# Two layers of spectral filter and bilinear unit on one core: who makes the first sums, smaller last steps, and a new order

## The chip, the cores and the metric

The kernel runs on one core of one Trainium2 chip. The metric is the device time of one execution in microseconds; a comparison takes the median of several runs. Engines: TensorE (PE in the profile) multiplies, VectorE (DVE), ScalarE (ACT) and GpSimd (POOL) work on elements, and SyncE (SP) issues nearly all transfers. Each engine does its instructions strictly in the order of its own queue.

## The reference

x has 2048 rows and 512 columns in float32. Twice over, two blocks are added to it:

```python
def _A_ref(x, w_r, w_i):
    X = rfft2(x, axes=(-2, -1))
    return irfft2(X * (w_r + 1j * w_i), s=(S, D), axes=(-2, -1))

def _B_ref(x, w_gate, w_up, w_down):          # F = 1792
    h = einsum("bsd,df->bsf", x, w_gate) * einsum("bsd,df->bsf", x, w_up)
    return einsum("bsf,fd->bsd", h, w_down)

x = x + _A_ref(layernorm(x), w_r0, w_i0)
x = x + _B_ref(layernorm(x), w_gate, w_up, w_down)
x = x + _A_ref(layernorm(x), w_r0, w_i0)      # the same weights again
x = x + _B_ref(layernorm(x), w_gate, w_up, w_down)
```

Both layers use the same weights. The layer norm has no scale and no shift.

## The kernel before, in words

x stays in SBUF for the whole run, as xs: 128 partitions, 16 tiles t of 512 columns. A layer goes through four stages.

*Forward.* For each tile t, `stats` and `rstd` make the reciprocal deviation rs (VectorE's bn_stats, two small steps on ScalarE, two on VectorE for each tile). Tiles are normalized in groups: the list G0 (line 18) gives the groups of the first layer, g2_ (line 1100) those of the second half between the layers. `fwd_rest` scales the twiddle tw by rs on ScalarE, folds the tile's columns on GpSimd (fo; tiles 2, 5, 8, 11 and 14 of layer 0 skip this and are combined by VectorE afterwards), multiplies (tp, eight matmuls), and copies the result into E. Tile 15, the last, is copied in two pieces, so that the groups that come first (FAST, line 104) need not wait for the whole.

*Middle.* E is worked through in 16 groups g. `middles` makes for each group a sum and a difference fs of two halves of E over all 16 tiles: on VectorE for the groups in FAST, on GpSimd for the others. CUTS (line 105) divides the sums of groups 0 to 2 into an early part (tiles 0 to 11) and a late one (12 to 15), so that the early part can be made before the last tiles are there. TensorE turns fs into features dp, ScalarE copies them to zs, TensorE multiplies across (zp), VectorE, ScalarE and GpSimd apply the filter (wq, loaded in eight pieces; jz and qp are its intermediate products), TensorE goes back (vq), and ScalarE stores into E. Groups are taken in pairs, (0), (1, 2), (3, 4) up to (15); dp of a pair is one step of 32 matmuls in the queue. A product without use (wp, "idle") stands between the last tile and the first features.

*Inverse.* For each tile `inv` multiplies (yi), forms vs, multiplies by the inverse twiddle (yo), and VectorE adds the result to xs in three steps. Then come the statistics of the second layer norm; `build_x` turns the normalized tiles (tq) and writes the operands xA and xS of the unit.

*Bilinear unit.* The hidden width is worked through in 14 slices ft, for the first eight tiles (h0 = 0) and the last eight (h0 = 8). `unit` forms gate and up products in a scheme with seven products instead of eight (gx, gy, gw, gz, gv), in one go of 512 columns (half = None) or in two halves of 256; a product is six matmuls. `down` forms the down products of two slices at once with seven products (ex to ez), and adds to xs. Where that scheme does not pay (first half of layer 0, and slices 0 and 1 at the end of layer 1), three matmuls db make each tile's down product directly, and VectorE adds it to xs (lines 868 to 887). The list seq (line 1029) says in which order slices come; the second half of layer 0 ends with slices 1 and 0 in halves, that of layer 1 with slice 1 whole and slice 0 in halves. The last eight tiles are stored at the end (lines 1110 and 1111), one transfer of 256 KB each.

*Order.* The functions only register operations. `Plan.order` sorts all 4887 of them by one written list: ORDER holds the sequence (as packed differences of indices), PLACES the buffer slot of each tile as it first appears. An engine's queue is the part of the sequence that belongs to it. The numbers called due have no effect on it. All instructions pass one helper, so the profile gives line 303 for every one; tiles are told apart by their names.

Of the kernel before, what the change touches and what calls it, by code (L numbers as in the profile page):

```python
# [17 lines left out]
G0 = [(0,), (1,), (2,), (3,)] + [(t, t + 1) for t in range(4, 16, 2)]  # L18
# [10 lines left out]
def consts():  # L29
# [74 lines left out]
FAST = (0, 1)  # L104
CUTS = {g: ((0, 12), (12, 16)) for g in range(3)}
# [6 lines left out]
UFIRST = 5.0  # L112
UNITS = ((7.5, 17.4, 15.0), (7.2, 16.9, 16.9)), ((7.2, 16.9, 14.5), (7.2, 14.5, 14.5))
# [3 lines left out]
    'c-l=`2Y3}#)1GtgO%Dkz5a|*+ibyp<igZMpNReW}f_zf^M35>dRT2FJ73?4&iV#phP(Tncbiqc6h#(y)0YV5#_RRmz>?ZzCp1pVP*;A*y^UiFDqNzMZQ68V<+vq%(p|f0)u5m2g#C6UjIzus'  # L117
    '(NQVC8YG}W~<){RmV1t%QxUTaRu8i+%Xi30ajx)Iwe&6IuxX<Gl++V=6V)(p^)^aqJvYF%xEZPgW3dK=1Doy7&9y64{h+SNpLYV0kTg+XKEP7SOo(z?vEBLfnV;QH|G?&H0sVy_lH`81U)un'
    'j4f%zQHVbM$0Er}7w`C0s0hLL44uR#m5d{?FeTmy4E?7uWcqNOx`W%G3|jybkq4(94q5xc6Q>;BAlWByo3p$5fbrsI4KJ?qkT^t>G_T;lRNe-=m5LF~IcBw)~UKiAjx9h^*`VeNPt4JjvL#S'
    'pcot1P=@UaRZ1r{$bvpaZNG#&1h|&{lv^W%x4Hp}9N)t#9Mp=XfPQh*>@U6H<$zT%5vEGMV5{WMJqXT)*pGEHqr1e&Xgh+d8fa87{}lX%uVIJz04K`iM@W@Wj$@{3u<7WUg{e8o?9v{066dj'  # L120
    'yKXmoi7J_s)O&^lpgxsv3JA`rEOdfmSLbdS?>d$uBVHq!}xqc_feYu;-ipi9`0vAFTMqppaERK??HmM<J8yr63fXOQEQ$?rLf=U`5jn~fy52X<2P}41{PKV`@CQGGFK%f`jhWi+J}A(agz4D'
    '4O%mLdU=vUr`hN@hFyw956ABxcqdNN88*SZ3~lA<N3_;bJ2QHv@zeNx4A&(*Igjg3)w9ey*t`$_=!f6CSfu@jn`#DgY2F!X2DM#O30-y<s4477)?LHWcPIPfJE*R9K+gB5loHjxrLDBt$*EM'
    'Fc0&URXuE^t$$TAcpvQ(-dppZct6|;?cy@(5>a!3e_6>gozsli#u>OZA9jks$W1OXl<{%%z7^fc4m-?y{+F@Vf6P01#&1fjkN83{L5+4{upRn|nS=#{x;#CWgG@WN+#R$3u-#icPdEA4tRol'
    'b0|8(`nZFqK-k74CD@IC|i@8TSeRJ;8Ot9I4<bofO>d{>9|dvLBIMh~i~GHr`qL-{*8in%vnw@snN2e>~hH=R6pks5Lz^h;ph>a*w=iv(`RZkOua(~xxxP8QZR53$JpaasTm`UUORAfb)e=_'
    'fkgLay?;h*I>7`S9E(^d^slO+vHmYvwhY0~?N^dUP4B3-~#Vc$1^3xypV!r&CY97i$^l>=G{_=SEOnJD$3Di+CKpj`n8g`Jn4=U&Z}g9t$sd2jeY0kGtaNVQCaBYAW}F_Zw=AS@(O7*-<POU'
    'PAYh5LkRe-EoY`H#1F?H=$rFy<|3ErW$;JAE8;mYlmOgToi>&UrvXX1R2E+4{=?L&&B-?ubE}O<{~kxf#=^zd1$T0g7ya~3iJPp>zo^GzQ*@`be^_)Einb!xFSYWpfdET8)ME=8U9DDcfNP8'
    'ZHfCi-hVB00{{4h%Nj#9@a%j18bIH{J4^EgoU9V>(Q}2&89eDj!(AsU{$=40k?bhMtmt}_Z@Cy#jwK2;G@{3*l;igC8ux;Y0`kn|H*J;|hZSz4vKY77g{cMB+y_rLz><?Li82vs#8wWHc%D@'
    'mKIE;i+t8yMpXW$(Ol`Lc_4FRJ(NvFrr5R?Sxe8CdSNmshk{?6daaeaeJwzGsQj0w??}g<)NtuXVhgtTq8|M*y);8ivGTRj@iIwUbSvMW~yWgBsyQ&KNw2C|i=$b~UYFWOI%3lJ_=EigiUKF'
    'BJkd;{0F?gc^nu=AgaE;AgT(?mKRpHHOzo8gah2G(*-dfugdbmgTX-qP7k%DKVSUjRT;;QtG;k(Q{{tY{xV<x#o_{9_>5$`)!jMB_qG|N3==JL~A+{k`ry5YL>Qt**mt|Hnl@@e==hDMa9+('
    '%f&(u=OSS?At1JKQ{4jNgm#v?cH&f)=@P#ui1YMQAV2x0|Cl(TDJNLmlY|dKvl_ekS<ThlaY|rj<(mVfTzlQyg!JIoGR?0|U|GqffFTRb>hV9wJ(6<+iEJ*YOh9!w70u)s;nh)v%UWMGfG>W'  # L130
    'kjYp8tvAZ8g8#SjP_C(KZz&fa~Gn12vT3pi*(k3{3(6GO~GmMF-se_(1=AESYmDEDtD@9W^*eN-eQB@V7HL*K@$zk7yOmhPk9E_=F#X=99k#|>3?XFsHV#_VU4+;>m2>uR&&++(mbVn=s4ev'
    'c}iLf<Vth3@O{WD1>JRZC2bYT^9<c(7MoqJCADxrnM^Jl(f-zAQ<IvyosfJb+R9~JZEFJgU^Hyk!0z4v*43weJPg<|*&Plg7W{zrfx!GQWtdzJxm+U_m+Z<~+1)-cIzyRWg2v}#q3&)2OElc'
    'UIo>tyZjXCyv9}58RSvkD0vZ0nMo%9_39h}};FY!wRWf^F<D<PNY%TbZVE@M~So;+`>kqG{l@XV`;#T7DW^N5O5ebb6YZcCu=*|L*_HzT^e1!F}evUT}y{pm`{@qKYu2y1ho|j@zbG*B5UeP'
    'sQ;#|+S!h7wHUUB&ABUWPFCJwvicE9%*eDiKAn#=G$4sCS4#NJj$`KXRufHl5iVY1h85<wsF{TW^lD>$&+>t^o;(<<%qSbDw#u2zc#QKw_{IGc)?H;@zE+{ldl2wLDh50tM1ANkD-Q)9c+>t'
    '|o_`q)VN#}f&Tu<v@q?T10Edzr>!j+wSUFQ!6o%5>9RE>FTrdm!_@c;3iXM2xBC=7q9>AKk$Q4Bbt`ymzeF{0MJ@ZR<tTzK|{Gi<U5Kz|d2k;QYOI6Xc$THkBN_;Y;sX>+==hxOdT%fjlnr5'
    'WCbHZ}%W35A$-lEY-BaQC`HX`P|wL(Y<ZLi1)o(c7R%20lfQ9^}TUke|smq{t5K@6*F}7viKISj4W5MhJ~SL;`1SDhq-dNtsRDup&)*RsI4b+eFyEVM9dPM@5lGE-ty1|C$kU0{EJv-nB|SZ'
    'D!=i=xI9HniJUU}Jb&T_nGTr$jIH3ELmVvUW!My2#YW?7s-o~o*jh6Gq-)%%_~Ns)-F#iWI80@{9g(Z@fljdQ8t`|YhlTY!moM=5?DIzp%(;d8>9`-}8o(EiXkOEqKUDrB?4@eJbgMu{!a>9'
    'r?opk;WU^f=aIj{GCdnq9=TR$u68z&W9&6gL(e*^Oy<u@jfI~j!JW1_z^bD>5-yO&^_=SMiBI@bqAmI0ZsVe`aoOGo2j-(knz5+6l8aUM&%69#f752f&jv|Kig`fW$qx`>K{0i{$I{4Z{;PS'
    '^24-GJ-G9|e^<~uwUol3u1)G@$>1aREbTnwj@Y^FW=nEjyUexm1ZG1Gmt2Dz2feBmrVpgq23;cTBH;_c;`oP)DRA$x64UGa1%3j()-u0CO31{ZMUE7vqs5iN7HmsQ+vNN;JTChWTfbnyiX4?'
    '2tQP;kC}?uv;7*1f^2;cL$#?@OfPx{FGD5=^)eeM~pqM4Us;u#P3_8+shr($Kb`N#w^Kv8V)P9vM8G-$D-KXV6{{>)!)M*{I{kqklOw5T9`x4SlWp`|^L|<k&+Jz9-=v64Cs8*JwWe8jaDjI'  # L140
# [132 lines left out]
def kernel(ctx: ExitStack, tc: tile.TileContext, x, wf, wc, wb, dfwd, tf, ti, mid, out):  # L273
# [733 lines left out]
    for layer in range(2):  # L1007
        dcs["i"] = load_di()
        idle(IDLE[layer])
        for gs in TWOS:  # L1010
            middles(gs, E, dcs["f"], W, lambda g: t0 + BOFF + BSTEP * g, SWAPS[layer])
# [156 lines left out]
```

## Time and profile before

| | |
|---|---|
| median of 3 runs | 1037.28 us (1037.04 to 1037.31) |
| the profiled execution | 1037.49 us |
| its span in the profile | 1035.7 us |
| TensorE busy | 1020.6 us, 99% |
| VectorE, GpSimd, ScalarE busy | 793.7, 745.8, 419.7 us |
| granted clock of TensorE | 1.00 throughout |

The span goes from the first to the last instruction of the trace; the device time holds a little more on either side. TensorE is the engine that is nearly always busy, so idle time on the others counts only where TensorE waits for them. Matmul ends are modelled and overlap a little: the distance from start to start is the better price of one.

### The profile page before, as it was taken

How to read it: one execution, taken by the hardware profiler on the slowest of the kernel's cores; microseconds unless marked ns; L12 is line 12 of the kernel's file. 1: busy time of each engine (PE TensorE's matmuls, PEld its weight loads, DVE VectorE, ACT ScalarE, POOL GpSimd, SP SyncE). 2: the span in 40 equal slices, each digit the busy share in tenths (PEclk: the TensorE clock that was granted, in tenths of full speed). 3: DMA queues.
4: the chain of work that ended last, by engine and by line, in shares of the span. 5: the costliest groups of instructions: out<-in, count | busy, mean ns of one | idle time of the engine just before them, and what ended most of it. 6: DMA issues, size and time to landing. Idle time of an engine off the chain costs nothing.

```text
span 1035.7 us, 18681 instructions
## 1 busy us (share of the span) xinstructions
PE 1020.6 (99%) x6544; PEld 878.8 (85%) x6544; DVE 793.7 (77%) x1533; ACT 419.7 (41%) x989; POOL 745.8 (72%) x950
## 2 busy tenths in 40 slices
PE   8999999999999999999999999999999999999998
PEld 6777988888888888889987789888888888888897
DVE  7779777678866677778878796888887766677788
ACT  6679534434432422332376693222333421222231
POOL 6968999999997675655798466554779953456571
PEclk9999999999999999999999999999999999999999
DMA  9720677767785675455290005536796365565442
GB/s 346 304 80 19 225 241 237 251 186 254 221 272 185 211 253 188 152 203 206 87 386 10 9 5 207 202 123 220 217 255 198 103 205 191 204 244 204 153 142 82
DMA packets 129468, 193.65 MB, mean 187 GB/s; under 512 B 39264, under 2 KB 50784, under 8 KB 127328
## 3 DMA queue, kind: packets, MB, share of 16 engines
q1 hardware_dynamic: 129232, 192.21, 55.1%
q8 instruction: 52, 0.85, 0.3%
q14 instruction: 40, 0.33, 0.1%
q10 hardware_dynamic: 144, 0.26, 0.1%
HBM read 145.52 MB, written 46.92 MB: 186 GB/s over the span
## 4 chain that ended last, share of the span: by engine, by line
PE 93%; DVE 4%; DMA 1%; ACT 1%; issue 1%; POOL 1%; SPq 0%; DVEq 0%; ACTq 0%
PE gz L303 15%; PE gx L303 15%; PE db L303 8%; PE gw L303 7%; PE gy L303 7%; PE gv L303 7%; PE ex L303 5%; PE ez L303 5%; PE ew L303 3%; PE dp L303 3%; PE zp L303 3%; PE ev L303 3%; PE vq L303 3%; PE ey L303 3%; PE tp L303 3%; DVE xs L303 2%
## 5 line engine op out<-in xcount | busy, mean ns | idle before, releaser
L303 PE MATMUL gx<-xA,wt 128*128 128x512 f32 (+1 forms) x756 | 175.5, 368 | 0.0
L303 PEld LDWEIGHTS gx<-xA,wt 128*128 128x128 f32 x756 | 130.4, 189 | 21.3 <-ACT s L303 0.2
L303 POOL TENSOR_TENSOR sf<-q,sf 128x256 fp32r<-128x256 f32 x99 | 73.2, 744 | 84.4 <-ACT sf L303 79.9
L303 POOL TENSOR_TENSOR sf<-cc,sf 128x256 fp32r<-128x256 f32 x97 | 72.1, 745 | 57.5 <-ACT sf L303 57.3
L303 DVE TENSOR_TENSOR xs<-xs,db 128x512 f32<-128x512 f32 x128 | 85.0, 681 | 24.3 <-PE db L303 23.9
L303 PE MATMUL db<-wd,h 128*128 128x512 f32 x336 | 89.5, 392 | 0.1
L303 PE MATMUL gz<-xS,wt 128*128 128x512 f32 (+1 forms) x378 | 88.3, 369 | 0.0
L303 PE MATMUL gy<-xS,wt 128*128 128x512 f32 (+1 forms) x378 | 88.2, 369 | 0.1
L303 PE MATMUL gz<-xA,wt 128*128 128x512 f32 (+1 forms) x378 | 88.1, 369 | 0.0
L303 PE MATMUL gw<-xS,wt 128*128 128x512 f32 (+1 forms) x378 | 87.8, 368 | 0.0
L303 PE MATMUL gv<-xS,wt 128*128 128x512 f32 (+1 forms) x378 | 87.5, 367 | 0.0
L303 ACT CAST sf<-q 128x256 fp32r<-128x256 f32 x99 | 39.9, 406 | 101.5 <-DVE q L303 53.7
L303 PEld LDWEIGHTS gv<-xS,wt 128*128 128x128 f32 x378 | 65.5, 189 | 11.1 <-issue 0.2
L303 PEld LDWEIGHTS gw<-xS,wt 128*128 128x128 f32 x378 | 65.4, 189 | 10.9
L303 PEld LDWEIGHTS gz<-xA,wt 128*128 128x128 f32 x378 | 65.0, 189 | 10.5
L303 PEld LDWEIGHTS gz<-xS,wt 128*128 128x128 f32 x378 | 64.8, 189 | 10.6
L303 PEld LDWEIGHTS gy<-xS,wt 128*128 128x128 f32 x378 | 64.8, 189 | 10.6 <-DVE cc L303 0.3
L303 PEld LDWEIGHTS db<-wd,h 128*128 128x128 f32 x336 | 62.5, 188 | 13.2 <-DVE xs L303 0.5
L303 ACT COPY s<-gx 128x512 f32<-128x512 f32 (+1 forms) x63 | 33.8, 536 | 96.8 <-PE gx L303 93.7
L303 DVE TENSOR_TENSOR q<-gy,s 128x512 f32<-128x512 f32 (+1 forms) x63 | 39.7, 630 | 39.6 <-PE gy L303 24.3
L303 POOL TENSOR_TENSOR wt<-rg,wt 128x512 fp32r<-128x512 f32 (+1 forms) x56 | 64.3, 1155 | 3.8 <-ACT wt L303 3.8
L303 PEld LDWEIGHTS ez<-bf,sf 128*128 128x128 f32 x402 | 56.3, 190 | 5.2 <-issue 0.7
(166 smaller groups left out, 2486.1 us busy)
## 6 DMA issues: line engine op xcount, KB each, us to landing
wt<-gu SPq DMA_DIRECT2D x36, 1024.0 KB, 7.3
wt<-gu SPq DMA_DIRECT2D x36, 768.0 KB, 6.2
bf<-dn SPq DMA_DIRECT2D x20, 1024.0 KB, 5.5
wq<-in_wf_dram SPq DMA_DIRECT2D x16, 1024.0 KB, 8.5
bf<-dn SPq DMA_DIRECT2D x20, 768.0 KB, 4.7
gu<-wt SPq DMA_DIRECT2D x14, 1024.0 KB, 6.3
gu<-wt SPq DMA_DIRECT2D x14, 768.0 KB, 6.0
rg<-in_wb_dram SPq DMA_DIRECT2D x14, 512.0 KB, 4.3
```

The costliest lines, as they stand in the source:

```text
L303: ins = f(*args, **kw)
```

## The change

Five things change, and the written order with them.

1. Tiles 14 and 15 are normalized singly instead of as a pair, in the prologue and between the layers. Each group has its own two steps on ScalarE.
2. FAST has group 2 as well: its sums go from GpSimd to VectorE. CUTS has one entry for each layer: in layer 0 the early part still ends at tile 12, in layer 1 at tile 10. The first piece of tile 15's copy holds three groups instead of two.
3. The second half of layer 0 ends with slice 1 whole (512 columns) and slice 0 in halves, as layer 1's does.
4. The down product of tile 15 in the very last unit is made in two halves of 256 columns, each with its own addition, and tile 15 is stored in two transfers of 128 KB.
5. ORDER and PLACES are new: 4879 operations. On TensorE, among other things: tile 2 goes ahead of tile 3 and tile 5 ahead of tile 4 in the prologue; in layer 1's middle the features of groups 1 and 2 come ahead of group 0's zp, where before they came behind it (in layer 0 they did already); in the inverse stages tiles 3 and 7 change places, and in layer 0 the first tile of the second half (t9) comes ahead of two tq. In the prologue ScalarE makes tile 2's rs ahead of tile 0's twiddle, and VectorE does group 0's late sums first and six sums of groups 1 and 2 behind them, while GpSimd's queue goes on with whole sums of groups 6, 5, 4, 5 and 6. At the end tile 15's two halves come ahead of tiles 14, 11, 8 and 10; before, the last ones were 8, 14, 10 and 11. SP's queue has many loads in other places.

```diff
-G0 = [(0,), (1,), (2,), (3,)] + [(t, t + 1) for t in range(4, 16, 2)]
+G0 = [(0,), (1,), (2,), (3,)] + [(t, t + 1) for t in range(4, 14, 2)] + [(14,), (15,)]
...
-FAST = (0, 1)
-CUTS = {g: ((0, 12), (12, 16)) for g in range(3)}
+FAST = (0, 1, 2)
+CUTS = [{g: ((0, at), (at, 16)) for g in FAST} for at in (12, 10)]
...
-        cuts = ((0, 2), (2, 16)) if t == 15 else ((0, 16),)
+        cuts = ((0, len(FAST)), (len(FAST), 16)) if t == 15 else ((0, 16),)
...
-            for lo, hi in CUTS.get(g, ((0, 16),)):
+            for lo, hi in CUTS[layer].get(g, ((0, 16),)):
...
-                def go(db=db, j=j, o=o + 128 * r):
+                def go(lo=0, hi=512, db=db, j=j, o=o + 128 * r):
                     w = wd()[:, ft % 2]
-                    mm3(db(), h()[:, j, 0, o:o + 128], h()[:, j, 1, o:o + 128], w[:, 0], w[:, 1], True, True)
+                    mm3(db()[:, lo:hi], h()[:, j, 0, o:o + 128], h()[:, j, 1, o:o + 128], w[:, 0, lo:hi], w[:, 1, lo:hi], True, True)
...
+                if last == "end" and t == 15:
+                    for lo, hi in ((0, 256), (256, 512)):
+                        pe(0.36, lambda lo=lo, hi=hi: go(lo, hi), r_, [(db, lo)], due=at)
+                        dve(256, lambda db=db, lo=lo, hi=hi: tt(xs[:, 15, lo:hi], xs[:, 15, lo:hi], db()[:, lo:hi], ALU.add), [(db, lo), ("xs", 15)], [("xs", 15, lo)], due=at + CLEAR)
+                    continue
...
-               *(((1, 0, 8), (0, 0, 8), (1, 1, 8), (0, 1, 8)) if layer == 0 else ((1, None, 8), (0, 0, 8), (0, 1, 8)))]
+        seq = [*START, *((ft, None, 0) for ft in range(2, 14)), *((ft, None, 8) for ft in range(13, 1, -1)), (1, None, 8), (0, 0, 8), (0, 1, 8)]
...
-            g2_ = [(8, 9), (12, 13), (10, 11), (14, 15)]
+            g2_ = [(8, 9), (12, 13), (10, 11), (14,), (15,)]
...
-            for t in range(8, 16):
+            for t in range(8, 15):
                 load(256, lambda t=t: SP.dma_start(out[:, t], xs[:, t]), [("xs", t)], [("out", t)], due=t0)
+            for lo, hi in ((0, 256), (256, 512)):
+                load(128, lambda lo=lo, hi=hi: SP.dma_start(out[:, 15, lo:hi], xs[:, 15, lo:hi]), [("xs", 15, lo)], [("out", 15, lo)], due=t0)
```

START only names the first four entries of seq, which are the same as before; `begun` counts an undivided slice as begun.

## Rows read from the trace of the kernel before

**Rows 1.** Page of the profile, part 1: busy us (share of the span) xinstructions.

```profile
PE 1020.6 (99%) x6544; PEld 878.8 (85%) x6544; DVE 793.7 (77%) x1533; ACT 419.7 (41%) x989; POOL 745.8 (72%) x950
```

**Rows 2.** What TensorE waited for: us in total, times, longest us.

```profile
PE tp L303 <- ACT rs L303: 1.7, 1, 1.7
PE zp L303 <- ACT zs L303: 1.4, 2, 0.7
...
PE tp L303 <- POOL fo L303: 0.9, 1, 0.9
PE tq L303 <- DVE xA L303: 0.9, 1, 0.9
```

**Rows 3.** Table by stretches: us, busy time of each engine, PEclk, DMA share, GB/s.

```profile
72.00:92.00 20.00, 17.99 (x106) 12.65 (x106) 19.29 (x62) 17.76 (x49) 18.23 (x23) 1.00 0.02 6
92.00:515.00 423.00, 422.89 (x2293) 366.87 (x2293) 316.23 (x592) 157.34 (x364) 344.43 (x404) 1.00 0.63 207
...
606.00:1000.00 394.00, 393.33 (x2299) 347.80 (x2298) 302.33 (x529) 125.42 (x301) 248.42 (x329) 1.00 0.57 188
```

**Rows 4.** Timeline of VectorE, 23 to 27: start us, us, line, operation, shape, count.

```profile
23.34 0.36 DVE L303 TENSOR_TENSOR fs<-E 128x192 f32<-128x192 f32 x1
...
24.29 0.74 DVE L303 TENSOR_TENSOR fs<-E 128x192 f32<-128x192 f32 x1
...
26.45 0.76 DVE L303 TENSOR_TENSOR fs<-E 128x64 f32<-128x64 f32 x1
```

**Rows 5.** Timeline of GpSimd, 24 to 29.

```profile
24.11 0.70 POOL L303 TENSOR_TENSOR fs<-E 128x192 f32<-128x192 f32 x1
...
27.68 1.42 POOL L303 TENSOR_TENSOR fs<-E 128x256 f32<-128x256 f32 x2
```

**Rows 6.** Timeline of TensorE, 26 to 32.

```profile
26.83 2.85 PE L303 MATMUL dp<-df,fs 128*64 128x128 f32 x48
29.50 1.99 PE L303 MATMUL zp<-zs,midt 128*64 128x256 f32 x12
```

**Rows 7.** Timeline of VectorE, 535 to 538.

```profile
535.65 1.45 DVE L303 TENSOR_TENSOR fs<-E 128x192 f32<-128x192 f32 x1
...
537.43 0.35 DVE L303 TENSOR_TENSOR fs<-E 128x64 f32<-128x64 f32 x2
```

**Rows 8.** Timeline of GpSimd, 535 to 539.

```profile
535.75 1.13 POOL L303 TENSOR_TENSOR fs<-E 128x192 f32<-128x192 f32 x2
537.80 0.83 POOL L303 TENSOR_TENSOR fs<-E 128x256 f32<-128x256 f32 x1 [0.92 <-ACT E L303]
```

**Rows 9.** Timeline of TensorE, 537 to 545.

```profile
537.81 1.10 PE L303 MATMUL dp<-df,fs 128*64 128x128 f32 x16
539.65 1.08 PE L303 MATMUL zp<-zs,midt 128*64 128x256 f32 x8 [0.74 <-ACT zs L303]
...
543.16 1.08 PE L303 MATMUL zp<-zs,midt 128*64 128x512 f32 x4 [0.68 <-ACT zs L303]
```

**Rows 10.** Timeline of TensorE: products of 512 and of 256 columns in layer 0.

```profile
452.97 1.55 PE L303 MATMUL gy<-xS,wt 128*128 128x512 f32 x6
454.36 1.52 PE L303 MATMUL gw<-xS,wt 128*128 128x512 f32 x6
...
483.24 0.88 PE L303 MATMUL gx<-xA,wt 128*128 128x256 f32 x6
483.96 0.88 PE L303 MATMUL gy<-xS,wt 128*128 128x256 f32 x6
```

**Rows 11.** Timeline of VectorE, 1025 to 1033.

```profile
1025.20 0.97 DVE L303 TENSOR_TENSOR hw<-q,hw 128x256 fp32r<-128x256 f32 x1
...
1031.96 0.69 DVE L303 TENSOR_TENSOR xs<-xs,db 128x512 f32<-128x512 f32 x1
```

**Rows 12.** Timeline of TensorE, 1025 to 1032.

```profile
1025.78 3.00 PE L303 MATMUL db<-hw 128*128 128x512 f32 x12
1029.28 2.65 PE L303 MATMUL db<-hw 128*128 128x512 f32 x9 [0.50 <-DVE xs L303]
```

More of the change, by code (lines that the diff above doesn't have):

```diff
@@ L121 @@
[L121 to L128, printed above, removed]
@@ L543, in features @@
                                   skip_group_check=True)
-        pe(0.83 * len(gs), features, [*((fs, i, lo) for g, fs in zip(gs, fss) for lo, _ in CUTS.get(g, ((0, 16),)) for i in range(2)), df, *(["idle"] if gs[0] == 0 else [])], dps)
+        pe(0.83 * len(gs), features, [*((fs, i, lo) for g, fs in zip(gs, fss) for lo, _ in CUTS[layer].get(g, ((0, 16),)) for i in range(2)), df, *(["idle"] if gs[0] == 0 else [])], dps)
         for g, dp in zip(gs, dps):
@@ L1010 @@
         for gs in TWOS:
-            middles(gs, E, dcs["f"], W, lambda g: t0 + BOFF + BSTEP * g, SWAPS[layer])
+            middles(gs, E, dcs["f"], W, lambda g: t0 + BOFF + BSTEP * g, SWAPS[layer], layer)
         t0 += COFF + BSTEP * 16
@@ L1028 @@
         t1 = t0 + FIRST
-        seq = [(0, 0, 0), (1, 0, 0), (0, 1, 0), (1, 1, 0), *((ft, None, 0) for ft in range(2, 14)), *((ft, None, 8) for ft in range(13, 1, -1)),
-               *(((1, 0, 8), (0, 0, 8), (1, 1, 8), (0, 1, 8)) if layer == 0 else ((1, None, 8), (0, 0, 8), (0, 1, 8)))]
-        begins = []
+        seq = [*START, *((ft, None, 0) for ft in range(2, 14)), *((ft, None, 8) for ft in range(13, 1, -1)), (1, None, 8), (0, 0, 8), (0, 1, 8)]
+        skip = 4 - len(START)
+        begins = [t1] * skip
         t = t1
-        for k, (ft, half, h0) in enumerate(seq):
+        for k, (ft, half, h0) in enumerate(seq, skip):
             begins.append(t)
@@ L1052, in second @@
             return st
-        for k, (ft, half, h0) in enumerate(seq):
+        for k, (ft, half, h0) in enumerate(seq, skip):
             if k == 4:
@@ L1081 @@
                         down_w(wd, f)
-                unit(X, ws[ft], wd, h, ft, half, h0, *begins[k:k + 3], None, i == 3 and ("end" if k + 1 == len(seq) else "down"))
+                unit(X, ws[ft], wd, h, ft, half, h0, *begins[k:k + 3], None, i == 3 and ("end" if k + 1 == len(seq) + skip else "down"))
             else:
-                first = ft // 2 not in blocks or (half is not None and (ft // 2, half) not in begun)
+                first = ft // 2 not in blocks or (half is not None and not {(ft // 2, half), (ft // 2, None)} & begun)
                 keep = "own" if first else True
```

142 lines of the change are left out of this document (76 added, 66 removed).

## The prediction, made before the changed kernel ran

> **What bounds the kernel now.** I read the page's busy list first, then TensorE's list of waits, then the table by stretches, and only after that the timelines of the few places where TensorE stands. TensorE is busy 1020.6 of 1035.7 us [rows 1], so 15.1 us are all that a new order can win without taking work off TensorE. The list of waits says where they lie [rows 2]: the first two layers' starts (a wait of 1.7 us for ScalarE's rs, two of 0.7 us for zs) and single waits of 0.9 us and less in the inverse transforms. The table by stretches [rows 3] shows the long middle as full: from 92 to 515 us TensorE misses 0.11 us, from 606 to 1000 us 0.67 us. In the inverse stretches VectorE is nearly full instead: 19.29 of 20 us from 72 to 92.
>
> All sums below are made against the profiled execution: 1037.49 us, 1.8 us more than its span, and 0.21 us above the median of 1037.28.
>
> **Part 1, the first sums of layer 0.** VectorE takes group 2's four sums from GpSimd. Before the last tile arrives three wide sums run on VectorE; the first takes 0.36 us, the last 0.74, because GpSimd works on group 2's wide sums at the same time (0.70 us each) [rows 4, 5]. With GpSimd idle there, the second and third fall to about 0.36 us: 2 x 0.39 = 0.78 us sooner. Tile 14's two additions, which stand behind them, move up too. Before that, the new order lets tile 2, which needs no fold by GpSimd, go ahead of tile 3 on TensorE; this fills most of the wait of 0.9 us for fo [rows 2]. But ScalarE now makes tile 2's rs pair ahead of tile 0's twiddle, which I put at 0.4 us against it. I take tile 15 to end 0.25 us sooner. The idle product waits for tile 14's bank, so group 0's features start near 26.1 instead of 26.83 [rows 6].
>
> Then cover is lost. After group 0's last sums VectorE still owes six sums for groups 1 and 2 (two wide, four narrow), where before it owed two, and GpSimd had finished group 2. GpSimd meanwhile has five whole-group sums in a row (groups 6, 5, 4, 5, 6), 0.70 us apart [rows 5], from about 25.4. A VectorE sum that meets a running GpSimd sum ends just behind it: the narrow one at 26.45 took 0.76 us [rows 4] beside one that ran from 26.40, while narrow ones alone take 0.35 us for two [rows 7]. A wide one also delays GpSimd: 0.83 us instead of 0.72 [rows 8]. One VectorE sum per GpSimd sum makes 25.4 + 2 x 0.83 + 3 x 0.70 = 29.2, and the sixth some 0.2 behind. The features of groups 1 and 2 then start near 29.4. Before they started 0.9 behind group 0's, at 27.7, without a wait (48 matmuls in 2.85 us, rows 6). That is +1.7; since one sum may slip in ahead of GpSimd's first, I take **+1.5**. Bounds: if VectorE's sums ran free (0.36 us wide, 0.14 narrow) they would end at 26.8, before TensorE comes, and the gain of 0.7 would stay; if GpSimd takes the port twice running, as at 535.75, where a wide sum of VectorE lasted 1.45 us beside two of GpSimd [rows 7, 8], it is +2.0.
>
> The Trainium skill has the rule for this: "SBUF — State Buffer", Who interferes with whom, says that a VectorE instruction with two SBUF inputs and a GpSimd instruction that reads SBUF exclude each other, and that whoever issues first keeps the port for its whole instruction. The row of 0.76 us agrees. The row of 1.45 us does not quite: a waiting VectorE sum was passed over once. By the rule alone the sum is the +1.7 above, by that row the +2.0.
>
> **Part 2, the first sums of layer 1.** Before, TensorE waits 0.74 us for zs of group 0 and 0.68 us for zs of group 2 [rows 9]. The new order puts the features of groups 1 and 2 between group 0's features and its zp, and the cut at tile 10 lets the early sums begin before the last tiles. Features cost 0.89 us a group, a zp 0.91: without waits group 2's zp would start at 537.81 + 0.89 + 0.91 + 1.78 = 541.39. It starts at 543.16, so 1.77 us are lost there. The early sums (six, 160 wide, an estimate of 0.3 us each between 0.36 for 192 and 0.14 for 64) have GpSimd idle, since group 2's sums (535.75 to 536.88, rows 8) no longer stand there, and end by 537.2. The late six (96 wide, near 0.19 us each) begin at 537.25. Three pass before GpSimd's first whole sum at 537.80; the fourth waits for it (0.83), the fifth for a 0.2 us step, the sixth for the next (0.70): 539.4. Features of groups 1 and 2 could have started at 538.70, so 0.7 of the 1.77 is lost again; what is late next is VectorE, not ScalarE: zs of group 0 is ready at 539.6 and now lies beside those features. **-1.1**, bounds -1.8 (no meeting) and +0.5 (GpSimd twice running at each of the last three).
>
> GpSimd's own queue loses four sums of 0.3 to 0.6 us before groups 3 and 4, so nothing behind it is later.
>
> **Part 3, the undivided unit.** Fourteen products of 256 columns, 0.72 us apart, become seven of 512, 1.36 to 1.39 us apart [rows 10]: 14 x 0.72 - 7 x 1.375 = 0.45 us off a stretch where TensorE is full. VectorE and ScalarE lose eight instructions. I take **-0.4**, bounds 0 (if a 512-column product ties up a bank that the next waits for) and -0.5.
>
> **Part 4, the end.** The halved product is not the last one. In the new order tile 15's halves are followed by whole products and additions for tiles 14, 11, 8 and 10; the last addition is still 0.69 us [rows 11] and the last store still 256 KB. So halving shortens nothing at the end; it costs VectorE 2 x 0.33 - 0.60 = 0.06 us and SP one more issue beside other work. What helps is the order. Before, tile 14's product waits 0.50 us for an addition [rows 12], and the last addition ends at 1032.65 [rows 11]. After, VectorE goes from 1023.5 (0.3 later than before, since the step of gv now stands ahead) through one step of its products (0.46), five additions 0.60 apart (tiles 12, 14, 13, 9, 12), two steps of 0.34, the hw step beside GpSimd (0.97, of which 0.90 counts), half of tile 15 (0.33) and the last hw step (0.34): 5.7 us, to 1029.2. The products of tiles 11, 8 and 10 wait for that step: three of 0.71 (twelve matmuls in 3.00 us are four products) [rows 12] and an addition of 0.69 give 1032.1 with the first one's start. **-0.5**, bounds -0.7 (no gap on VectorE) and +0.1.
>
> **Parts without a term.** Tiles 14 and 15 normalized singly add two ScalarE steps (0.29 and 0.20 us) in the prologue and at the layer's turn, on an engine busy 17.76 of 20 us at worst [rows 3]; tile 14 gets its twiddle sooner, and the steps lie beside TensorE's other tiles. Uncovered they cost 0.5 us. The inverse stretches keep VectorE's work; new neighbours on TensorE (t7 and t3 changed places, a tile of the second half between) only move where it waits: the 0.88 us before tq [rows 2] goes, and the operands come later by as much. I take **+0.1** for both, bounds +-0.6. In the middle, loads change places in SP's queue, but stay more than 5 us of TensorE's work ahead of their readers: 0, bounds -0.3 and +0.5.
>
> **Sum:** +1.5 - 1.1 - 0.4 - 0.5 + 0.1 = -0.4: 1037.1 for a profiled execution, **1036.9** for a median. Its own range is 1035.4 to 1038.6.
>
> **Rivals.** (a) VectorE's sums run free, or GpSimd starts its row later than I think: -0.7 - 1.7 - 0.4 - 0.5 + 0.1 = -3.2, **1034.1**. For it: GpSimd's sum at 537.80 took 0.83 instead of 0.72 [rows 8], so there VectorE came first. Against it: the sums that met a running one waited for its end [rows 4, 7]. (b) Slower: GpSimd takes the port twice running in both layers. Then the first features of groups 1 and 2 stand +2.0 in layer 0 and +0.5 in layer 1, with -0.4, 0 at the end and +0.6 in the inverse stages: +2.7, **1040.0**. It decides where group 2's features start after 541 in layer 1. For it is the one row of 1.45 us; against it that GpSimd's row has short steps between. (c) The inverse stage, where VectorE is full, takes back what layer 1's start wins: the -1.1 is gone, **1038.0**. Against it: the four sums that leave GpSimd free both engines' meeting point there.
>
> **How the numbers follow.** My forecast 0.56, (a) 0.24, (b) 0.12, (c) 0.08. A measurement of this kernel can tell 0.2%, 2.1 us, from no change: faster is below 1035.2, slower above 1039.4. Of the forecast 0.07 lies below 1035.2 and 0.01 above 1039.4; of (a) 0.21 is faster, of (b) 0.09 slower. So faster 0.28, the same 0.62, slower 0.10. The range leaves out the lower half of (a) and most of (b): 1034.4 to 1039.2.
>
> **What would show it.** In the new profile: a wait before the features of groups 1 and 2 of 1.5 to 3 us in layer 0, with VectorE's sums 0.7 us apart; none above 1 us in layer 1 and no wait for zs there; the last addition a whole one, ending 2 to 3 us before the end. I am wrong if layer 0's features start without a wait (then rival a), or if layer 1's start wins nothing.

## The result, and the profile after

The changed kernel takes 1040.1 us in the median (1038.78 to 1042.87, 8 runs), the kernel before 1037.19 us in the same session. The ratio is 1.003, 95% interval 1.0019 to 1.0041: slower by 0.3%, where 1036.9 us and a range up to 1039.2 were forecast. The profiled execution of after took 1038.78 us and is the lowest of the eight; its span is 1037.0 us against 1035.7 before. So 1.3 us are to be found by comparing the two traces; another 1.3 us (1040.1 against 1038.78) stand in the other executions and not in this trace.

Busy time of the engines, from the page (busy us, share, instructions). TensorE is not busier than before [rows 1]; it only stands longer:

```profile
PE 1020.0 (98%) x6505; PEld 876.9 (85%) x6505; DVE 799.3 (77%) x1535; ACT 420.1 (41%) x992; POOL 743.7 (72%) x942
```

What TensorE waited for in after (us in total, times, longest us). Against [rows 2], both waits for zs are gone, and so is that for fo; new are 2.1 us for VectorE's first sums (fs), 1.0 us for the load bf and 0.6 us for a copy by ScalarE (E). Three grew: the first wait of the prologue for ScalarE from 1.7 us (for rs) to 2.3 (for tws, the twiddle scaled by rs), that of a yi for an addition (xs) from 0.5 to 1.2 us, and that of a db for an addition from 0.5 to 0.8:

```profile
PE tp L304 <- ACT tws L304: 2.3, 1, 2.3
PE dp L304 <- DVE fs L304: 2.1, 1, 2.1
...
PE yi L304 <- DVE xs L304: 1.2, 1, 1.2
PE ex L304 <- DMA bf<-dn: 1.0, 1, 1.0
PE yo L304 <- DVE rs L304: 0.9, 1, 0.9
PE db L304 <- DVE xs L304: 0.8, 1, 0.8
PE yo L304 <- DVE vs L304: 0.7, 1, 0.7
PE tp L304 <- ACT E L304: 0.6, 1, 0.6
```

The table by stretches (us, then busy time of PE, PEld, DVE, ACT, POOL, then PEclk, DMA share, GB/s). The row from 606 to 1000 us, which missed 0.67 us before [rows 3], misses 1.70; the wait of 1.02 us for the load is the difference:

```profile
606.00:1000.00 394.00, 392.30 (x2296) 346.75 (x2296) 303.96 (x528) 125.84 (x302) 249.40 (x329) 1.00 0.58 187
```

Layer 0's middle, timelines of VectorE, GpSimd and TensorE in turn (start, us, engine, line, operation, shape, count; in brackets the idle time before and what ended it). Nine sums of VectorE take 4.36 us; the fourth to the eighth run in step with GpSimd's five whole sums, each ending 0.08 to 0.21 us behind one of them, and the ninth alone; TensorE stands for 2.07 us ahead of the features of groups 1 and 2 [rows 4 to 6]:

```profile
24.41 4.36 DVE L304 TENSOR_TENSOR fs<-E 128x192 f32<-128x192 f32 x9
...
24.89 3.66 POOL L304 TENSOR_TENSOR fs<-E 128x256 f32<-128x256 f32 x5 [3.59 <-DVE fs L304]
...
24.59 1.10 PE L304 MATMUL wp<-midt 128*128 128x512 f32 x2 [0.46 <-ACT E L304]
25.62 1.10 PE L304 MATMUL dp<-df,fs 128*64 128x128 f32 x16
28.78 1.97 PE L304 MATMUL dp<-df,fs 128*64 128x128 f32 x32 [2.07 <-DVE fs L304]
30.55 2.01 PE L304 MATMUL zp<-zs,midt 128*64 128x256 f32 x12
```

Layer 1's start, the same three timelines. GpSimd has one whole sum where it had group 2's before it [rows 7, 8]; TensorE runs through, with 0.16 us where it waited twice for zs [rows 9]:

```profile
536.74 2.11 DVE L304 TENSOR_TENSOR fs<-E 128x160 f32<-128x160 f32 x6
539.28 1.64 DVE L304 TENSOR_TENSOR fs<-E 128x96 f32<-128x96 f32 x6 [0.44 <-ACT E L304]
...
539.80 0.83 POOL L304 TENSOR_TENSOR fs<-E 128x256 f32<-128x256 f32 x1 [2.31 <-ACT E L304]
...
539.81 1.10 PE L304 MATMUL dp<-df,fs 128*64 128x128 f32 x16
541.07 1.97 PE L304 MATMUL dp<-df,fs 128*64 128x128 f32 x32 [0.16 <-PE dp L304]
542.84 1.95 PE L304 MATMUL zp<-zs,midt 128*64 128x256 f32 x12
```

The undivided products, the turn between the layers, the late load and the end on TensorE, then VectorE's last additions [rows 10 to 12]:

```profile
480.65 1.52 PE L304 MATMUL gx<-xA,wt 128*128 128x512 f32 x6
...
526.54 0.95 PE L304 MATMUL ev<-bf,sf 128*128 128x256 f32 x6
528.09 1.13 PE L304 MATMUL tp<-tw,fo 128*128 128x128 f32 x8 [0.60 <-ACT E L304]
529.11 0.95 PE L304 MATMUL ez<-bf,sf 128*128 128x256 f32 x6
...
787.11 0.95 PE L304 MATMUL ex<-bf,sf 128*128 128x256 f32 x6 [1.02 <-DMA bf<-dn]
...
1027.20 0.88 PE L304 MATMUL gx<-xA,wt 128*128 128x256 f32 x6
1027.91 1.21 PE L304 MATMUL db<-hw 128*128 128x512 f32 x6
1029.88 3.39 PE L304 MATMUL db<-hw 128*128 128x256 f32 x15 [0.76 <-DVE xs L304]
...
1030.54 0.42 DVE L304 TENSOR_TENSOR xs<-xs,db 128x256 f32<-128x256 f32 x1 [0.38 <-PE db L304]
1031.24 2.75 DVE L304 TENSOR_TENSOR xs<-xs,db 128x512 f32<-128x512 f32 x4 [0.28 <-PE db L304]
```

I read the shift of TensorE's start at equal work, after minus before, through the two traces (where after has one tile's forward product more behind it, that tile's 0.89 us are taken off, an eighth of what eight of them in a row take): -1.21 us at the idle product ahead of layer 0's features, **+1.02** at the features of groups 1 and 2, still +1.00 at 519.7, **+2.00** behind the turn between the layers (the first features of layer 1 start at 539.81 against 537.81), **+0.55** at the zp of group 2 in layer 1, +0.40 at 602, **+1.41** behind the load at 787, and +1.3 at the end.

### The profile page after: what moved, and what is told of

It is laid out like the page before. It is cut to its first block, busy times and chain, and to the rows that moved or that the text cites. A ratio compares the mean times of both kernels' runs of the same rounds, so it can differ in the third digit from the quotient of the medians.

```text
span 1037.0 us, 18597 instructions
## 1 busy us (share of the span) xinstructions
PE 1020.0 (98%) x6505; PEld 876.9 (85%) x6505; DVE 799.3 (77%) x1535; ACT 420.1 (41%) x992; POOL 743.7 (72%) x942
## 4 chain that ended last, share of the span: by engine, by line
PE 92%; DVE 5%; DMA 1%; ACT 1%; POOL 0%; issue 0%; DVEq 0%; ACTq 0%
PE gz L304 15%; PE gx L304 14%; PE db L304 8%; PE gw L304 7%; PE gv L304 7%; PE gy L304 7%; PE ex L304 5%; PE ez L304 5%; PE ew L304 3%; PE vq L304 3%; PE dp L304 3%; PE zp L304 3%; PE ey L304 3%; PE ev L304 3%; PE tp L304 2%; DVE xs L304 2%
## 5 line engine op out<-in xcount | busy, mean ns | idle before, releaser
L304 POOL TENSOR_TENSOR sf<-q,sf 128x256 fp32r<-128x256 f32 x91 | 67.5, 745 | 94.5 <-ACT sf L304 77.2
L304 POOL TENSOR_TENSOR sf<-cc,sf 128x256 fp32r<-128x256 f32 x109 | 81.1, 747 | 54.2 <-ACT sf L304 54.0
L304 DVE TENSOR_TENSOR xs<-xs,db 128x512 f32<-128x512 f32 (+1 forms) x129 | 86.0, 678 | 20.5 <-PE db L304 20.3
L304 ACT CAST sf<-q 128x256 fp32r<-128x256 f32 x91 | 36.5, 406 | 102.0 <-DVE q L304 51.7
L304 ACT CAST sf<-cc 128x256 fp32r<-128x256 f32 x109 | 43.9, 406 | 72.8 <-PE ew L304 22.8
```

Source lines behind the costliest of these rows:

```text
L304: ins = f(*args, **kw)
```

## The experiments

There were twelve runs, the first of them after itself. Unless said otherwise each of the others changes the written order alone, so the diffs show queues; times are medians, and each ratio, with its 95% interval, is to the kernel before in the same session (1037.40 us in the session of the first four runs, then 1037.34 for four, 1037.38 for three and 1037.67 for the last). An interval is about 0.9 us wide to either side, so a difference between two of these kernels that is smaller than that is read from the traces or not at all.

**After once more** (no edit).

> The changed kernel again, to see a second execution. Two theories for the 2.9 us that it loses. D: a load of the down weights (bf) near 787 us, queued on SP behind the small transfers of the second half's tiles, lands after its product is due, by an amount that changes from run to run. S: VectorE's first sums, which now meet GpSimd's, change from run to run. D expects a wait for bf between 0 and 5 us, other than the 1.02 us of the first profile, and starts of the features of groups 1 and 2 within 0.2 us of 28.8 and 541.1. S expects these starts to move by 0.5 us or more and the wait for bf to stay near 1.0. Both: median between 1039.0 and 1041.5.

Measured: 1039.82 us, 1.0025 (1.0016 to 1.0034). It is the base for the rest. The signs of D came (bf waits 0.4 us, and the first sums run as they did), but its profiled execution shows something that neither theory had. The same 2.07 us wait stands ahead of the features (28.91 us here), but behind it TensorE's granted clock falls from 2.4 to 1.2 GHz for a while; the table by stretches (columns as above; PEclk is third from the end), then TensorE's timeline:

```profile
28.00:30.00 2.00, 1.08 (x14) 1.11 (x16) 1.00 (x4) 0.00 (x0) 1.61 (x5) 0.83 1.00 401
30.00:32.00 2.00, 2.00 (x23) 2.00 (x21) 0.00 (x0) 0.00 (x0) 2.00 (x4) 0.50 0.99 410
32.00:34.00 2.00, 2.00 (x15) 1.26 (x14) 0.00 (x0) 1.56 (x3) 0.16 (x1) 0.82 1.09 423
...
28.91 3.35 PE L304 MATMUL dp<-df,fs 128*64 128x128 f32 x32 [2.07 <-DVE fs L304]
32.00 2.28 PE L304 MATMUL zp<-zs,midt 128*64 128x256 f32 x12
34.08 1.94 PE L304 MATMUL dp<-df,fs 128*64 128x128 f32 x32
```

From the features to the next features 5.17 us pass (34.08 - 28.91) against 3.61 in after's first trace (28.78 to 32.39): 1.56 us lost to the clock.

**Layer 1's four turns of tile 11 ahead of other loads** (queue of SyncE, ahead of the late bf; turns are transfers of 64 KB that carry parts of a normalized tile, xf are transfers of 256 KB that read them back).

```diff
-xf t13, xf t9, turn t11.1, turn t11.2, turn t11.0, xf t15, bf p5, turn t11.3
+turn t11.1, turn t11.2, turn t11.0, turn t11.3, xf t13, xf t9, xf t15, bf p5
```

> The changed kernel with one edit in SP's queue: the four small transfers of tile 11 in layer 1 stand ahead of the three loads of xf (tiles 13, 9 and 15), as before the change, so that they are gone when the load of bf is issued. D (late load): the wait of 1.02 us for bf near 787 falls under 0.2, the median falls by 1.0 to 2.5 us against the changed kernel of the same call, and its runs lie within 1 us instead of 4. S (first sums) and any other place: no change beyond 0.4 us.

Measured: 1040.01 us, 1.0026 (1.0016 to 1.0037). The wait for bf stayed (0.9 us): the turns themselves had to wait for their transposes until 776.26, bf was issued at 780.56 and landed in 6.9 us. A miss: it moved the lateness from the landing to the issue, and the median did not move.

**Layer 0's sums of group 2 back to GpSimd**, with their places in the queues.

```diff
-                    if g in FAST:
+                    if g in FAST and (layer, g) != (0, 2):
```

> The changed kernel with the four first sums of group 2 of layer 0 back on GpSimd (ahead of its whole sums), and group 1's second wide sum on VectorE ahead of the narrow ones; layer 1 stays changed. If the lock step of VectorE's sums with GpSimd's is what holds the features of groups 1 and 2: they start near 26.7 instead of 28.78, the wait of 2.07 us falls under 0.4, and 1.5 to 2.0 us are won against the changed kernel. Rival: GpSimd is nearly full there (31.97 of 36 us from 24 to 60), so what it takes over comes back as later sums of groups 3 to 6, and less than 0.6 us is won.

Measured: 1037.89 us, 1.0004 (0.9995 to 1.0012). The 2.07 us wait is gone; TensorE's timeline has all three features in one row. Those of groups 1 and 2 start at 27.84, 0.94 us ahead of after's and 1.1 us later than expected, because the prologue ran 0.4 us later in this trace and VectorE, which now meets GpSimd earlier, brings the idle product 1.02 us later in all:

```profile
25.61 1.10 PE L304 MATMUL wp<-midt 128*128 128x512 f32 x2 [1.11 <-ACT E L304]
26.63 3.18 PE L304 MATMUL dp<-df,fs 128*64 128x128 f32 x48
```

So part 1 holds most of the loss: 1.9 us of the median (1039.82 against 1037.89 in one session) for 0.94 us in the trace.

**Layer 1's sums of group 2 back to GpSimd** (the same edit with `(1, 2)`).

> The changed kernel with the four first sums of group 2 of layer 1 back on GpSimd, all else as changed. Theory A, that layer 1's start wins by the order of TensorE's steps alone (features of groups 1 and 2 ahead of group 0's zp): zp of group 2 starts within 0.3 us of 543.7 and the time stays within 0.4 us. Theory B, that it wins because VectorE makes these sums: the features of groups 1 and 2 wait 0.7 to 1.5 us more, and the time rises by as much.

Measured: 1039.37 us, 1.0024 (1.0015 to 1.0033). In this trace zp of group 2 starts at 544.55, against 543.72 in after, but TensorE had already lost 0.80 us at 256; from the idle product of layer 1 to that zp 4.93 us pass here and 4.91 in after. So that VectorE makes group 2's sums gives nothing there. What is left for layer 1's gain is TensorE's order (features of groups 1 and 2 ahead of the first zp) and the cut at tile 10; neither was put back alone. The median is 0.45 us lower, within the noise. What was lost at 256 was a second late transfer, a down product that waited 0.70 us for an addition:

```profile
256.40 0.98 PE L304 MATMUL db<-wd,h 128*128 128x512 f32 x3 [0.70 <-DVE xs L304]
```

Followed back, it is VectorE waiting 1.31 us for xn (253.86), ScalarE waiting 3.95 us to cast the weights of slice 11 (251.69), and their load rg, issued at 245.73 behind two xf, two sets of turns and a tw, and landed 5.9 us later; in the kernel before it was issued at 244.26, ahead of them, and landed in 4.3 us.

**Loads.** rg of slice 11 ahead of two entries of SyncE's queue; ScalarE's two casts of it behind tile 9's xn; layer 1's turns of tile 11 behind bf.

```diff
-xf t8, turn t13.1, ..., rg ft11        (SyncE, layer 0)
+rg ft11, xf t8, turn t13.1, ...
-wt ft11 x2, rs t14, xn t9              (ScalarE)
+rs t14, xn t9, wt ft11 x2
-turn t11 x4 around xf t15, bf p5       (SyncE, layer 1)
+xf t15, bf p5, turn t11 x4
```

> The changed kernel with three edits for loads alone: in layer 0 the load rg of slice 11 ahead of two transfers (turns of tile 13, xf) on SP, and ScalarE's two steps that read it behind the normalization of tile 9; in layer 1 all four small transfers of tile 11 behind the load of bf (half 0, slices 10 and 11). L (late loads cost the median about 1 us, in amounts that change): the waits near 255 us (db, 0.1 to 0.8 in five profiles) and 787 us (0.3 to 1.0) fall under 0.1 and 0.2; the median falls by 0.7 to 1.3 us. Rival K (granted clock): the falls of the clock after the wait of 2.1 us in layer 0 are what makes the runs differ, so the median falls by 0.5 at most and the runs still lie 3 us apart, with mean clocks of 0.998.

Measured: 1039.21 us, 1.0018 (1.001 to 1.0027). The wait near 255 us is gone and bf waits 0.3 us, but 0.8 us came back further on, for wt at 796.57. In five of the eleven executions the mean clock was 0.997 or 0.998. The median fell by 0.6 us, less than the intervals can tell. The traces tell more about the first wait than about the second. Near 255 us six of the nine other traces whose queue there is that of after wait 0.2 to 1.0 us, and none of the three with this edit does. For bf five of the nine traces with after's queue at 787 us wait 0.3 to 1.2 us, and two of the three with this edit wait 0.3. Nor did the turns behind it make bf land soon, as the link of this trace's chain shows (start, us, what):

```profile
778.55 7.74 DMA bf<-dn
```

**The wait filled** (four products of the idle kind that nothing reads, between group 0's features and those of groups 1 and 2 in layer 0; this kernel does more work than the reference needs).

```diff
+            if layer == 0 and gs == (0,):
+                idle(2, "fill")
```

> The changed kernel with four more products without use (512 columns of midt, the same bank as the idle product) between the features of group 0 and those of groups 1 and 2 in layer 0. They fill the wait of 2.07 us and take nothing that waits. K (the clock falls to 1.2 GHz behind that wait in about half of the runs and gives back 1.6 us late): the features of groups 1 and 2 still start near 28.9, a wait of 0.1 to 0.5 is left, no stretch from 24 to 60 has a clock under 1.00, and the median falls by 0.6 to 1.2 us. L (late loads alone): no change beyond 0.4 us.

Measured: 1038.69 us, 1.0012 (1.0003 to 1.002). VectorE's sums take as long as in after, and the features are as late (29.25; 0.37 us of the delay stand already at the idle product), but TensorE works until then and the clock stays at 2.4 GHz:

```profile
27.01 2.31 PE L304 MATMUL wp<-midt 128*128 128x512 f32 x4
29.25 1.97 PE L304 MATMUL dp<-df,fs 128*64 128x128 f32 x32
```

Work without use makes the kernel 1.1 us faster than after (1038.69 against 1039.82). Against after's first session, each as a distance from its kernel before, it is 1.6 us. I take 1.1 us as the clock's share of the median. The executions of the five kernels with the wait say the same: within each, those with a mean clock of 0.998 or less are 0.9 to 2.0 us slower in the median than the others.

**GpSimd later** (its two small steps wq, which wait for VectorE's hp behind the ninth sum, ahead of its five whole sums of groups 4 to 6).

```diff
-fs g6.0, g5.0, g4.0, g5.1, g6.1, wq.1, wq.0      (GpSimd)
+wq.1, wq.0, fs g6.0, g5.0, g5.1, g6.1, g4.0
```

> The changed kernel with GpSimd's two small filter steps (wq of hp, which wait for VectorE's step on hp behind its last first sum) ahead of its five whole sums in layer 0, and group 4's first sum behind those of groups 5 and 6. Nothing else moves; the same sums on the same engines, but VectorE's end before GpSimd's begin. P (lock step of the two engines): VectorE's nine last sums end near 26.3 instead of 28.77, the features of groups 1 and 2 start near 26.6 without a wait, and 2.0 to 2.4 us are won in the profile, 2.2 to 3.3 in the median if the clock's falls go with the wait. Rival: GpSimd is the bound of this stretch, its sums for groups 5 and 6 are late by 1.5 us, and at most 1.0 us is won. Second rival: VectorE's sums are long by themselves (0.7 us each beside nothing), then nothing is won.

Measured: 1036.64 us, 0.9994 (0.9985 to 1.0003). VectorE's nine sums take 1.70 us, not 4.36, and TensorE runs through the features 2.12 us earlier than in after (26.66, the first 16 of the 48 end there). Timelines of VectorE, GpSimd and TensorE:

```profile
24.52 1.70 DVE L304 TENSOR_TENSOR fs<-E 128x192 f32<-128x192 f32 x9
...
26.39 0.38 POOL L304 TENSOR_TENSOR wq<-wq,hp 128x8 f32<-128x8 f32 x2 [4.91 <-DVE hp L304]
26.72 6.22 POOL L304 TENSOR_TENSOR fs<-E 128x256 f32<-128x256 f32 x9
...
25.73 2.84 PE L304 MATMUL dp<-df,fs 128*64 128x128 f32 x48
28.41 1.99 PE L304 MATMUL zp<-zs,midt 128*64 128x256 f32 x12
```

GpSimd's later start costs nothing that TensorE shows. With the clock, the meeting of the two engines is worth 3.2 us of the median (1039.82 - 1036.64), and this kernel is 2.05 us faster than the filled one of the same session, as much as the wait is long.

**All repairs together** (GpSimd later, loads, the turn and the end as in the runs below).

> All repairs together: GpSimd's sums later, the three load edits, in the turn between the layers ScalarE's copy of tile 6 ahead of two other steps (TensorE waits 0.8 us there for its bank), and at the end tile 14's product ahead of tile 15's second half. If the parts add up: 2.2 (first sums) + 0.9 (clock) + 0.8 (loads) + 0.8 (turn) + 0.2 (end) = 4.9 us less than the changed kernel, near 1035.0, runs within 1.5 us: faster than both. If later stretches take it back (the inverse stages, full on VectorE): near 1036.5.

Measured: 1035.61 us, 0.9986 (0.9977 to 0.9995): faster than both kernels, 4.2 us less than after where 4.9 were expected. Its interval lies below 1; of the others only those of the next run and of the end do.

The last four take these repairs apart, on the base of "GpSimd later".

**Loads on that base.**

> The kernel of e6_pool_later (GpSimd's five whole sums behind VectorE's late sums) plus the three moves of loads of e4_loads, nothing else. On this base the granted clock did not fall, so the loads can be read by themselves. Theory L (late loads hold TensorE near 255 us and near 787 us in a part of the executions): the wait of 0.8 us of a down product for an addition, 240 to 270 us, is gone from the profile, no wait for bf above 0.3 us near 787, and the median is 0.5 to 1.0 us below e6_pool_later's 1036.64: 1035.6 to 1036.1. Rival N (the waits only move: the stretch behind them takes them back): the wait near 255 is gone, but the median stays at 1036.4 to 1036.9.

Measured: 1036.23 us, 0.9988 (0.998 to 0.9997). The wait near 255 is gone, bf waits 0.3 us. The median fell by 0.4 us, between the two theories and within the noise.

**The turn, ScalarE** (its copy of tile 6 moved up, to behind the first squares of tile 13).

```diff
-squares t13, ac t13, cast, squares t13, rs t13, tw t9, rs t13, cast, E t6
+squares t13, ac t13, E t6, cast, squares t13, rs t13, tw t9, rs t13, cast
```

> The kernel of e6_pool_later with one move: between the layers ScalarE's copy of tile 6 stands behind its instructions for tile 13. Theory S (the 0.60 us that TensorE waits there for ScalarE at 526.75 is the queue's order alone): that wait is gone and TensorE is 0.5 us or more earlier at layer 1's start, median 1036.0 to 1036.3. Rival V (VectorE is as late at that place): the wait for ScalarE is gone, one of 0.5 us for VectorE's rs stands in its place, and the median stays within 0.2 us of 1036.64.

Measured: 1036.57 us, 0.9994 (0.9986 to 1.0003). Rival V: the wait for ScalarE went and one for VectorE took its place. (This trace has no wait near 255, where its base lost 0.76 us, and stands that much earlier throughout; at layer 1's start it is 0.72 us ahead, so the move gave nothing.)

```profile
525.38 1.13 PE L304 MATMUL tp<-tw,fo 128*128 128x128 f32 x8
527.05 0.95 PE L304 MATMUL ez<-bf,sf 128*128 128x256 f32 x6 [0.54 <-DVE rs L304]
```

**The end** (tile 14's product, addition and store ahead of tile 15's second half).

```diff
-db t15 (256:512), db t15 (0:256), db t14, db t11, ...
+db t15 (256:512), db t14, db t15 (0:256), db t11, ...
```

> The kernel of e6_pool_later with one move at the end: tile 14's down product, addition and store go ahead of tile 15's second half. Theory H (VectorE's addition for the first half of tile 15's bank makes TensorE wait 0.76 us there, and the time goes through to the end): no wait above 0.2 us after 1020, the last addition ends 0.7 us sooner, and the median is 1035.9 to 1036.1. Rival K (the last store's landing sets the end, not the addition): the wait is gone and the median stays within 0.2 us of 1036.64.

Measured: 1035.98 us, 0.999 (0.9981 to 0.9999), 0.66 below its base: theory H. The medians alone could not tell, but the trace shows the same 0.67 us. TensorE's last products run in one row, VectorE's last five additions too, and from the start of gx to the end of the last addition 6.12 us pass (1024.39 to 1030.51) against 6.79 in after (1027.20 to 1033.99):

```profile
1024.39 0.88 PE L304 MATMUL gx<-xA,wt 128*128 128x256 f32 x6
1025.11 4.68 PE L304 MATMUL db<-hw 128*128 128x512 f32 x21
...
1027.27 3.24 DVE L304 TENSOR_TENSOR xs<-xs,db 128x512 f32<-128x512 f32 x5
```

**The turn, TensorE** (with the move on ScalarE: tile 0's forward product to behind the down product that writes ev).

```diff
-tp t5, tp t0, ez, ex, tp t6, ex, ey, ew, ev, tp t9, ez
+tp t5, ez, ex, tp t6, ex, ey, ew, ev, tp t0, tp t9, ez
```

> The kernel of e9_pool_turn with one move on TensorE: tile 0's forward product at the turn between the layers goes from in front of the turn's last five down products to behind the one that writes ev, so that two forward products (tiles 0 and 9) lie between that and the last one, which writes ez, as they do in the kernel before (there tiles 6 and 9). ScalarE's copy of tile 0 follows it. Theory F (the last product waits for the bank that VectorE frees with its addition of ev, in the kernel before too, where it starts 0.14 us behind that addition; what the new order lost is the tile that filled this time): the wait of 0.54 us ahead of ez is gone or below 0.2, the product starts 0.5 us or more earlier than e9_pool_turn's 527.05, and the median is 1035.8 to 1036.2. Rival G (VectorE's queue is what is late over the whole turn): the other products of the turn then wait for VectorE or GpSimd instead, the sum of waits at the turn stays, and the median stays within 0.2 us of e9_pool_turn's 1036.57.

Measured: 1037.88 us, 1.0003 (0.9994 to 1.0012). Rival G, and worse: the wait ahead of the last ez went, but the products ahead of it now wait for ScalarE. The product of ez starts at 527.79 against 527.05; that difference is what this trace had lost near 255 us (0.75), so the move itself neither won nor lost up to there. By layer 1's start another 1.0 us is lost, most of it ahead of the last forward product.

```profile
519.59 0.95 PE L304 MATMUL ez<-bf,sf 128*128 128x256 f32 x6 [0.18 <-ACT sq L304]
...
522.57 0.97 PE L304 MATMUL ex<-bf,sf 128*128 128x256 f32 x6 [0.41 <-ACT u L304]
...
537.53 1.13 PE L304 MATMUL tp<-tw,fo 128*128 128x128 f32 x8 [0.77 <-issue]
```

## Why the prediction was wrong

The three signs that it named all came: a wait of 1.5 to 3 us in layer 0 (2.07) with VectorE's sums one to each of GpSimd's, no wait for zs in layer 1, and a whole last addition 3 us before the end. What failed is what it had priced at nothing or nearly so: the clock behind the new wait, the loads and the turn between the layers. Against the profiled execution, in us, forecast and measured:

| term | forecast | measured |
|---|---|---|
| layer 0 up to the features of groups 1 and 2 | +1.5 | +1.02 |
| layer 1's start | -1.1 | -1.45 |
| undivided unit | -0.4 | -0.1 |
| end | -0.5 | -0.06 |
| inverse stretches and singles | +0.1 | -0.15, and +1.00 at the turn |
| loads in the middle | 0 | +1.02 |
| sum | -0.4 | +1.3 |

**Part 1, right in mechanism.** The step "one VectorE sum per GpSimd sum" is shown by the pair after and "GpSimd later": the same nine sums, 4.36 us beside GpSimd and 1.70 us without. The rule of the Trainium skill that the prediction weighed ("SBUF — State Buffer", Who interferes with whom) fits: each of five VectorE sums waited for one GpSimd sum and none for two, so the row of 1.45 us [rows 7] found no second one. The size was too high because GpSimd's row began at 24.89, not 25.4. The prologue had gained more than I took: group 0's features start 1.21 us earlier, at 25.62 against 26.83, where I took 0.7. Rival (a), sums that run free, is excluded.

**The step that failed first: the sum has no term for what the new wait does to the clock.** The trace of before could not show it: it has no such wait there, and its clock was 1.00 in every stretch of [rows 3]. A wait of 2.07 us was counted as 2.07 us less what it replaced; in the second trace of after the work behind it took 1.56 us more at 1.2 GHz. The kernel after, in both sessions, and the three that keep that wait (turns, layer 1's sums, loads) had a mean clock of 0.998 or less in 25 of 48 executions; the filled one and "GpSimd later" in none of 22. The wait is not the only place for it: layer 0's sums back, without the wait, had 2 of 11, the five kernels built on "GpSimd later" 6 of 56, and the kernel before 1 of 107. Share of the median: 1.1 us (after against the filled one). Without it the time would have lain just inside the range.

**The step "loads stay more than 5 us of TensorE's work ahead of their readers: 0" failed in what it counts.** It counts from the issue, and what a reader waits for is the landing. For bf of 1 MB near 787 us the trace of before has the issue at 778.39 and the landing 7.2 us later, near 785.6. Its reader starts behind that, 0.92 us after the product ahead of it, which takes 0.71 where nothing is late:

```profile
785.70 0.95 PE L303 MATMUL ex<-bf,sf 128*128 128x256 f32 x6
```

So the margin was gone already in the kernel before. In after the load is issued at 778.72, 7.2 us ahead of when its reader is due (7.1 before), and lands 8.3 us later; in the chain that ended last it stands as a link of its own (start, us, what):

```profile
778.72 8.26 DMA bf<-dn
```

In the nine traces with after's queue at this place it landed 6.5 to 8.6 us behind its issue. So the 1.02 us of the table is one draw of the landing against no margin, and that the new order of SyncE's queue lengthened it is not shown: with the turns of tile 11 moved behind it, it still took 7.7, 7.7 and 5.7 us. The other late load, rg of slice 11 near 245 us, did move: the new order issues it 1.4 us later (245.70 against 244.26), behind smaller transfers, where TensorE is 1.0 us late, and ScalarE's queue waits for it. What both cost in the median is not settled: the two experiments on loads won 0.6 and 0.4 us, each less than the noise.

**The turn between the layers had no term but +0.1.** It lost 1.0 us: the shift went from +1.00 to +2.00. The two repairs (ScalarE's copy, TensorE's tile) each removed the wait that the trace named and got another for it, so the named wait was not the cause; VectorE and ScalarE are late there together. Which of their instructions sets it, the two singly normalized tiles among them, was not tried alone and stays open.

**Part 2 was right, for one of its reasons.** -1.45 against -1.1; the experiment with layer 1's sums back on GpSimd shows that group 2's sums on VectorE give nothing, so that TensorE's order gives it is inferred, with the cut at tile 10 untested beside it. Rivals (b) and (c) are out. The measured 1040.1 is (b)'s time, but by luck: (b) has +2.0 and +0.5 at the two layers' starts, and they showed +1.02 and -1.45. Against (c), the inverse stage behind layer 1's start took nothing back: the shift went from +0.55 to +0.40 across it.

**Part 4 failed in the path.** I had TensorE's last three products wait for VectorE's last hw step, and that step end at 1029.2. It ended at 1030.17, which is 1028.76 without the 1.41 us that after was late by then, 0.4 us sooner than I had it, because the hw step that I took as held up by GpSimd (0.90 us, from [rows 11]) took 0.42. But the products did not follow it. TensorE waits earlier, for 0.76 us until 1029.88, because the second half of tile 15 waits for VectorE's addition of the first half; behind that half tile 14's product comes as well. So tile 11's product, with which my sum goes on at that step, started at 1031.05. I had counted the halves' 0.06 us on VectorE and not that wait. Moving tile 14's product between the halves wins 0.67 us in the trace. **Part 3** won 0.1 of its 0.4 us; two gaps near 502 us take 0.23 us of the rest (products 0.85 and 0.82 us apart instead of 0.72). It was not tried alone.

The fixed terms and the clock do not fill the median. The trace sums to +1.3 us; with the loads at 0.5 instead of 1.02 (an estimate from the two experiments) and the clock at 1.1 it is 1.9 us, while the medians say 2.4 (second session) and 2.9 (first). The rest of 0.5 to 1.0 us is not placed. There are two candidates. The first wait of the prologue, for tws, goes from 1.1 to 3.2 us in the traces of the changed kernels. And the trace of after has nearly none of the wait near 255 us that six of the nine others show. They were not separated.

## What to carry to other kernels

When work moves to an engine that shares something with another, read what the other has queued at that time, and move that first: here two small steps of GpSimd, put ahead of its sums, moved more time (3.2 us) than the whole change did (2.4 to 2.9). A new wait on TensorE is to be priced twice, once by its length and once at the lower clock for the work behind it, even if no trace of before shows that clock. A load's margin is to be counted from its landing, load by load, and not from its issue; a load that lands just in time in one trace can be late in the next, since a single trace shows only one draw of the landings. Where two traces are compared far into a kernel, take off first what one of them had lost before.

## What the runs showed of the hardware

- TensorE's granted clock fell from 2.4 to 1.2 GHz behind a wait of 2.07 us in one trace of after and not in the other, with the same wait; the work behind it cost 1.56 us more. With four products without use in the gap the mean clock was 0.999 or 1.0 in all 11 executions. It fell too in the trace of the loads on the base of "GpSimd later", behind a first wait of 3.2 us in the prologue: 0.88 from 8 to 12 us and 0.69 from 12 to 16.
- Nine two-input sums on VectorE: 1.70 us alone, 4.36 us with five of them beside GpSimd's sums. GpSimd's own slowed little: the five took 3.66 us, 0.71 or 0.72 us each, and 0.83 or 0.84 where a wide sum of VectorE went ahead.
- The same load of 1 MB (bf near 787 us), at the same place of the same queue, landed 6.5 to 8.6 us behind its issue in nine traces; the median of all bf loads of this size in the trace of after is 5.5 us.
